# Centring a weight with SCALAR_TENSOR_TENSOR in place of TENSOR_TENSOR, and the builder's estimates with it

## The chip, the cores and the metric

The kernel runs on one core of a Trainium2 chip. The metric is the device time of one execution in microseconds (us), the median of several runs. A profile of one execution shows what each engine did: PE (matmuls; PEld, its weight loads), DVE (VectorE), ACT (ScalarE), POOL (GpSimd), and SP, which issues most of the DMAs.

## What is computed

Nystrom attention over 8 batches of 8 heads (576 tokens, head size 64, 32 landmarks), followed by a normalised two-layer network with a residual. Cut to what matters:

```python
A, Bm, C = softmax(q @ k_lm.T), softmax(q_lm @ k_lm.T), softmax(q_lm @ k.T)
Z = Bm.T / (norm1(Bm) * norminf(Bm) + 1e-6)
for _ in range(6):
    Z = 2 * Z - Z @ Bm @ Z
x = heads_side_by_side(A @ Z @ C @ v)              # 8 x 576 x 512
xn = (x - mean(x)) / sqrt(var(x) + 1e-6) * g_ln
out = x + relu(xn @ w_ch1) @ w_ch2                 # 512 -> 2048 -> 512
```

The mean of x is never taken off x. It is taken off the weight: from each column of W1 (already scaled by g_ln) its mean over the 512 inputs is subtracted. This is "centring W1".

## The kernel before

**Tiling.** Tokens stand in 36 blocks of 128. W1 is held as `w1_16`, f16, 128 partitions by 4 input chunks by 2048; W2 as `w2_16`. The first layer of a batch has 16 chunks `m` of 128 hidden units (`First.chunk`), each 8 matmuls of 288 columns into a PSUM tile `psh`, and ACT or DVE writes its relu as `hT`. The second layer has 16 matmuls of 512 columns for each block (`bank<-w,hT` in the profile), and DVE writes them scaled and added into `xblk`; from batch 4 on seven products of half size take the place of eight.

**Centring.** The negative column means come from matmuls with a constant (`less_mean`, L1111) and lie as f16 tiles `less`. For batches 0 and 1, whose first layers come before the weight is centred, the means are added later, into the product `m16` (L1151 to L1157). When batch 1 takes its four products, `whole.extend` (L1159) puts eight jobs in a list: four column groups `f`, each in two halves of two input chunks. `center_w1(f, c)` (L1123) does one of them: one DVE instruction over 128x1024 f16, in place, `w1_16 + less`. Batches from 2 on use the centred weight. In the profile these are the rows `w<-w,less`.

**POOL's work beside it.** For each tile of q and k of a later batch POOL casts the staged f32 data to f16 (`nat`, 128x1152). For some of them it also makes landmark sums, in three halving sums `asum` and a last one `s`: four instructions behind the cast, here called a chain (`Coming.cast`, L778). DVE transposes `s` to `sT` and reduces it to `part`, and PE spreads `part` over the heads (`part,spread`) for the next attention. POOL also multiplies the exponentials of q's scores by their reciprocal sums (`normalize`, L512, rows `ea<-ea,lns`), and casts v (`natv`). PE uses `ea` in the matmuls `zcbd,ea` and in `psh<-ea,m`.

**What sets the order.** All engines run instructions in the order in which they are issued, and this order is made when the kernel is built. Four streams of work (attentions, first layers, rows of batch 0, second layers) are generators that say from when their next piece could run. `run` (L1512) takes the first that is ready by the clock of the builder, and `help_out` (L1427) puts side work between: loads, POOL's casts and chains, DVE's transposes, `center_w1` (L1467), measuring, stores. The clock is a set of estimates: `Clock.took` (L124) says how long an instruction takes on its engine, `Clock.note` (L146) moves the time at which the engine is free. For a DVE instruction over 1024 elements the estimate is 1080 ns (L141). When such an instruction writes `w1_16`, POOL's time of being free is also moved, by 430 ns (L205, with the names in `parted_w1`, L374). The estimates are used when the order is made and nowhere else; on the chip only semaphores hold an instruction.

A helper issues nearly all instructions, so most rows of the profile have its line: L268 for DVE, ACT and POOL, L274 for the matmuls. Rows are told apart by tile names.

## Time and profile before

| | |
|---|---|
| median of 3 runs | 281.72 us (281.32 to 282.81) |
| the profiled execution | 282.81 us, its span 281.0 us |
| PE, DVE, ACT, POOL busy | 266.2, 212.3, 161.9, 160.1 us |
| granted TensorE clock | 0.997 of full speed |
| `w<-w,less` on DVE | 8 instructions, 7.1 us, from 69.3 to 78.2 us |

The span goes from the first to the last instruction that the profile shows; the 1.8 us beside it lie around them. A row of a group gives engine, operation, output and inputs by tile name, their shapes and the count, then the busy time in us, the mean of one in ns, and the idle time of the engine just before, with what ended it. A row of the timeline gives start and length in us and merges equal neighbours. A row of a stretch gives its limits, its length, the busy time and count for PE, PEld, DVE, ACT and POOL, then granted clock, DMA share and GB/s.

### The profile page before, as it was taken

The numbers are of one execution on the slowest core, as the hardware profiler recorded it, in microseconds if no ns is written. First come the engines' busy times: TensorE is split into PE (matmuls) and PEld (weight loads), VectorE is DVE, ScalarE is ACT, GpSimd is POOL, SyncE is SP. The second block draws the span as 40 slices with busy tenths as digits, with TensorE's granted clock in tenths as the row PEclk, the third lists the DMA queues.
The fourth block names the chain that finished last, engine by engine and source line by source line (L and its number), as shares of the span: only waits on it lengthen the run. The fifth ranks groups of instructions, "written<-read, shape, count | busy, mean of one in ns | idle before, by whom it ended". The sixth has DMA issues, their size and how long they took to land.

```text
span 281.0 us, 8678 instructions
## 1 busy us (share of the span) xinstructions
PE 266.2 (95%) x3618; PEld 165.6 (59%) x3618; DVE 212.3 (76%) x479; ACT 161.9 (58%) x287; POOL 160.1 (57%) x187
## 2 busy tenths in 40 slices
PE   7988999999999999889989999999999999999994
PEld 7744554355444564344555645567877666678883
DVE  3558985999999847888978384697885499748761
ACT  2676954368554887148889754698248733671000
POOL 5368778999999999978999999310000040100000
PEclk9999999999999999999999999999999999999998
DMA  7999999989745579893750101310060005300606
GB/s 244 384 387 388 388 388 392 354 278 266 246 126 160 152 249 304 265 279 95 221 188 2 34 8 45 72 40 0 2 144 9 1 5 118 72 0 2 149 22 167
DMA packets 23375, 46.70 MB, mean 166 GB/s; under 512 B 2212, under 2 KB 2472, under 8 KB 23336
## 3 DMA queue, kind: packets, MB, share of 16 engines
q1 hardware_dynamic: 23176, 46.02, 51.9%
q8 instruction: 28, 0.46, 0.7%
q10 hardware_dynamic: 160, 0.13, 0.2%
q14 instruction: 11, 0.09, 0.1%
HBM read 36.70 MB, written 9.44 MB: 164 GB/s over the span
## 4 chain that ended last, share of the span: by engine, by line
PE 79%; DVE 9%; ACT 5%; issue 3%; DMA 2%; SPq 0%; DVEq 0%; ACTq 0%
PE bank L274 51%; PE psh L274 21%; DMA stg<-in_q_dram 2%; ACT hT L268 2%; DVE xblk L268 2%; PE pscv L274 2%; DVE m L268 2%; DVE xT L268 1%; PE psec L274 1%; PE psd L274 1%; DVE part L268 1%; ACT ec L268 1%; DVE hT L268 1%; ACT lns L268 1%; PE psea L274 1%
## 5 line engine op out<-in xcount | busy, mean ns | idle before, releaser
L274 PE MATMUL bank<-w,hT 128*128 128x512 f16 (+1 forms) x528 | 109.2, 335 | 1.1 <-issue 1.0
L268 ACT ACTIVATE hT<-psh 128x576 f16<-128x576 f32 x115 | 71.0, 652 | 17.4 <-PE psh L274 16.0
L274 PE MATMUL psh<-ea,m 128*128 128x288 f16 x512 | 76.9, 286 | 2.8 <-ACT hT L268 2.1
L274 PEld LDWEIGHTS <-hT 128*128 128x128 f16 x656 | 60.4, 98 | 32.2 <-issue 6.9
L274 PEld LDWEIGHTS <-m 128*128 128x128 f16 x512 | 47.9, 97 | 25.3 <-issue 10.1
L268 DVE SCALAR_TENSOR_TENSOR xblk<-bank,rstd,xblk 128x256 f32<-128x256 f32 (+1 forms) x77 | 39.2, 541 | 18.2 <-PE bank L274 18.2
L268 POOL TENSOR_TENSOR ea<-ea,lns 128x576 f16<-128x576 f16 x14 | 18.1, 1306 | 47.2 <-ACT lns L268 47.0
L268 POOL CAST nat<-stg 128x1152 f16<-128x1152 f32 x28 | 32.6, 1181 | 2.0 <-DMA stg<-in_k_dram 1.1
L268 POOL CAST natv<-stg 64x1152 f16<-64x1152 f32 (+1 forms) x23 | 26.7, 1161 | 8.8 <-DMA stg<-in_v_dram 7.9
L268 ACT COPY xblk<-bank 128x512 f32<-128x512 f32 (+1 forms) x34 | 19.1, 588 | 12.2 <-PE bank L274 12.0
L268 DVE BATCH_NORM_STATS2 six<-xblk 128x6 f32<-128x512 f32 x36 | 24.2, 671 | 0.0
L268 ACT CAST m<-bank 128x512 f16<-128x512 f32 x30 | 17.0, 588 | 9.9 <-PE bank L274 9.9
L268 DVE STREAM_TRANSPOSE xT<-nat 128x576 uint32<-128x576 uint32 x28 | 21.4, 765 | 0.6 <-POOL nat L268 0.6
L268 ACT ACTIVATE lns<-psd 128x576 f32<-128x576 f32 x16 | 10.3, 646 | 17.8 <-PE psd L274 16.7
L268 DVE TENSOR_REDUCE part<-xT 128x32 f16<-128x576 f16 x28 | 20.0, 742 | 0.2
L268 POOL TENSOR_TENSOR asum<-asum 128x256 f32<-128x256 f32 (+1 forms) x28 | 18.0, 644 | 2.2
L268 DVE CAST m<-bank 128x512 f16<-128x512 f32 x18 | 12.2, 679 | 7.3 <-PE bank L274 7.2
L268 POOL TENSOR_TENSOR asum<-nat 128x512 f32<-128x512 f16 x14 | 16.5, 1178 | 1.1
L274 PE MATMUL bank<-w2mix,hT 128*128 128x256 f16 x128 | 16.5, 273 | 0.0
L274 PE MATMUL bank<-w2mix 128*128 128x256 f16 x128 | 16.0, 273 | 0.0
L268 DVE SCALAR_TENSOR_TENSOR st<-st,bank 128x128 f16<-128x128 f16 (+2 forms) x36 | 11.1, 308 | 6.4 <-PE bank L274 6.0
L274 PE MATMUL bank<-zcbd,ea 128*128 128x256 f16 (+1 forms) x80 | 14.4, 275 | 1.0 <-DVE m L268 0.8
(123 smaller groups left out, 341.6 us busy)
## 6 DMA issues: line engine op xcount, KB each, us to landing
stg<-in_q_dram SPq DMA_DIRECT2D x16, 576.0 KB, 5.7
stg<-in_k_dram SPq DMA_DIRECT2D x16, 576.0 KB, 5.4
stg<-in_v_dram SPq DMA_DIRECT2D x16, 576.0 KB, 7.1
out_dram<-xblk SPq DMA_DIRECT2D x70, 128.0 KB, 2.3
wstg<-in_moe_w_ch_dram SPq DMA_DIRECT2D x16, 512.0 KB, 7.1
out_dram<-xblk ACTq DMA_DIRECT2D x2, 64.0 KB, 2.3
out_dram<-xblk SPq DMA_DIRECT2D x2, 64.0 KB, 2.1
g_rows<-in_moe_g_ln_dram SPq DMA_DIRECT2D x1, 2.0 KB
```

Source lines behind the costliest of these rows:

```text
L268: return lambda *args, **kw: keep(getattr(self.engine, op)(*args, **kw))
L274: keep(nc.tensor.matmul(o, l, r, start=start, stop=stop, tile_position=(rb, cb), skip_group_check=(skip or cb != 0)))
```

## The change

One instruction is written in another way: the same in-place sum, as SCALAR_TENSOR_TENSOR, that is `(w1_16 * 1.0) + less`. The builder's estimate of a DVE instruction over 1024 elements goes from 1080 to 1200 ns. The charge of 430 ns to POOL goes, and the set of names that served it. The second-layer mixes keep their own estimate of 690.

```diff
-    parted, mixed_, parted_w1 = {}, set(), set()
+    parted, mixed_ = {}, set()
...
             if n == 1024:
-                return 690 if name_of(i.outs[0].bass_ap) in mixed_ else 1080
+                return 690 if name_of(i.outs[0].bass_ap) in mixed_ else 1200
...
                 self.free[e] = done - self.OVERLAP[e]
-                if e == 'DVE' and count[0] == 1024 and writes[0] in parted_w1:
-                    self.free['Pool'] = max(self.free['Pool'], start) + 430
...
-    parted_w1.update(f"{w1_16.name}:{i}" for i in range(KCH * MCH))
...
         o = w1_16[:, ds(c, 2), ts(f, 512)]
-        dve.tensor_tensor(out=o, in0=o, in1=less(f)[:, None, :].broadcast_to([P, 2, 512]),
-                          op=ALU.add)
+        dve.scalar_tensor_tensor(out=o, in0=o, scalar=1.0,
+                                 in1=less(f)[:, None, :].broadcast_to([P, 2, 512]),
+                                 op0=ALU.mult, op1=ALU.add)
```

Since the estimates set the order, the order of all five engines differs from the first of these instructions on, in places.

## The prediction

> **What bounds the kernel now.** I read the busy table and the chain that ended last, then the busy times by stretch and the waits of 69 to 106 us, where the edited instructions lie, and then DVE and POOL there in order of time.

> ```profile
> PE 266.2 (95%) x3618; PEld 165.6 (59%) x3618; DVE 212.3 (76%) x479; ACT 161.9 (58%) x287; POOL 160.1 (57%) x187
> PE 79%; DVE 9%; ACT 5%; issue 3%; DMA 2%; SPq 0%; DVEq 0%; ACTq 0%
> ...
> 69.00:82.00 13.00, 12.69 (x245) 6.19 (x243) 12.40 (x28) 7.82 (x15) 12.21 (x13) 1.00 0.69 216
> 82.00:94.00 12.00, 12.00 (x111) 5.55 (x104) 10.81 (x27) 6.12 (x13) 11.29 (x15) 1.00 0.52 163
> ```

> PE is the bound: 95% of the span and 79% of the chain. In the last two rows (stretch, its length, then PE, weight loads, DVE, ACT, POOL) PE is full, but so are DVE (12.40 of 13.00) and POOL (12.21). POOL is nowhere in the chain: it is just in time. So a faster POOL gains little by itself, and a later DVE or POOL shows once its margin is gone. PE issues in a fixed order, so a late operand stops everything behind it.

> The edited instructions, and POOL beside them:

> ```profile
> L268 DVE TENSOR_TENSOR w<-w,less 128x1024 f16<-128x1024 f16 x8 | 7.1, 922 | 0.0
> L268 DVE TENSOR_TENSOR w2mix<-w2mix,hT 128x1024 f16<-128x1024 f16 x8 | 5.4, 681 | 0.0
> L268 DVE SCALAR_TENSOR_TENSOR xblk<-bank,rstd,xblk 128x512 f32<-128x512 f32 x19 | 13.9, 737 | 6.0 <-PE bank L274 6.0
> ...
> 69.35 3.49 DVE L268 TENSOR_TENSOR w<-w,less 128x1024 f16<-128x1024 f16 x4
> ...
> 69.43 2.02 POOL L268 TENSOR_TENSOR asum<-asum 128x256 f32<-128x256 f32 x2
> 71.53 0.75 POOL L268 TENSOR_TENSOR s<-asum,nat 128x128 f16<-128x128 f32 x1
> 72.23 1.60 POOL L268 CAST nat<-stg 128x1152 f16<-128x1152 f32 x1
> ...
> 80.91 1.26 POOL L268 TENSOR_TENSOR asum<-asum 128x256 f32<-128x256 f32 x2
> 82.24 0.43 POOL L268 TENSOR_TENSOR s<-asum,nat 128x128 f16<-128x128 f32 x1
> 82.63 2.52 POOL L268 TENSOR_TENSOR ea<-ea,lns 128x576 f16<-128x576 f16 x2
> ```

> The same DVE shape takes 681 ns on w2mix, with POOL nearly idle, and 922 on W1. POOL's pair of sums takes 2.02 us beside the W1 adds and 1.26 later, the last sum 0.75 against 0.43. The two engines block each other in turns. Over all eight adds POOL loses 0.76 + 0.32 + 0.46 + 0.72 + 0.56 + 0.33 = 3.15 us.

> **The change, part by part.**

> *The instruction.* Eight TENSOR_TENSOR go, eight SCALAR_TENSOR_TENSOR of 128x1024 come, both big operands in SBUF. The trace has none like that. Bounds: below, 681 ns, if it still takes two f16 elements at a time; above, the slope of SCALAR_TENSOR_TENSOR with a PSUM operand, 477 ns for 256 and 737 for 512, so 1.016 ns an element and 737 + 520 = 1257 ns for 1024. The f16 form with PSUM (732 for 512, 476 for 256) has the same slope. I take 1257: all rows of this operation lie on that line. That is 0.575 us more for each.

> [...]

> *Does it hold POOL?* Bounds: no hold at all, or for its whole length. The nearest row is not the W1 add but an add that goes one element at a time, also with two SBUF operands:

> ```profile
> 21.95 1.20 POOL L268 TENSOR_SCALAR w<-wstg,g_sb 128x512 f16<-128x512 f32 x1
> ...
> 21.86 0.81 DVE L268 TENSOR_TENSOR ea<-ea,lns 128x288 f16<-128x288 f16 x2
> ```

> Two such adds last from 21.86 to 22.67 (450 ns for 288 elements each, the slow rate). POOL's scaling, which elsewhere takes 0.69, takes 1.20 beside them: it ends 0.48 after the second add. So the slow rate does not spare POOL, and I take a hold for the whole length. [...]

> With the hold, each of the eight POOL instructions beside W1 is released 0.575 us later: 8 x 0.575 = **4.6 us** that POOL is later than before at 82.6.

> *The order.* The estimate goes from 1080 to 1200 and the 430 that POOL was charged for each add is gone, so the builder believes POOL to be earlier. Set side by side, the two built orders hold the same PE instructions, as many as before; up to the W1 adds nothing moves. Three moves matter. (1) On POOL the two ea products of batch 2 stood behind two sum chains (cast, three sums, last sum); now a third chain stands ahead of them. That chain lasts from 85.09 to 89.26, **4.17 us**. (2) On PE the last part/spread pair before batches 3 and 4 moves up to behind 12 psh matmuls. (3) One adding of W1 and the transposes change places on DVE, and PE's w2 matmuls are shared out anew between the six iterations. Loads and stores on SP change places from the same region on; their transfers are not in the chain there, so I cost them at nothing. If that cover fails a load of 5.4 us could show.

> *What PE then waits for.* The ea products end at 85.15 before; now at 85.15 + 4.6 + 4.17 = 93.9. PE wants them (times from its rows in order of time) at the first zcbd,ea matmul: 88.80 before, and one w2 matmul (0.22) more ahead of it now, 89.0. **Stall 4.9 us.**

> Next, POOL has two chains of 4.17 to the last sum that part needs: 93.9 + 8.3 = 102.2; transpose 0.23, reduce 0.28 and 0.13 to PE (reduce ended at 100.30, PE began at 100.43) make 102.85. PE, from zcbd at 93.9, needs 4.49 to the first w1 group (88.80 to 93.29 before, the same matmuls), then 0.34 + 0.99 (8 psh) + 0.87 (4 w2) + 0.49 (4 psh), which is 101.1. **Stall 1.75 us.**

> DVE itself is late too: the first four take 4 x 1.18 (1257 less the usual 0.08 overlap) in place of 3.49 less 0.06 and wait for POOL between them as now (1.1 us), so rsum starts at 69.35 + 4.72 + 1.1, about 75.1 and not 72.78. PE's gram follows rsum by 1.23 as before, 76.3, where PE is there after 7 w2 matmuls, 72.98 + 7 x 0.216 = 74.5: 1.8 late. In the iterations behind it each added instruction and its wait for POOL (1.2 to 1.6 us) stands ahead of one st, and PE has 4 to 8 w2 matmuls (0.9 to 1.7) to cover it; following both lists on, I find 0.4, 0.1 and 0.3 more. So PE is late by some 2.6 us at pszt. This lies ahead of the ea wait and within it: PE must wait until 93.9 anyway. So nothing is added; if the ea wait went, these 2.6 would show instead.

> Sum: 4.9 + 1.75 = 6.65, about **6.6 us**. Behind 106 us POOL is 4.4 us late and PE 6.6, so POOL has margin again (it waited 1.94 for lns at 127). The profiled execution took 282.81 with a span of 281.0; with 6.6 it would be 289.4. The median of the three runs is 281.72: forecast **288.3**.

> Both ends of this case: if each hold grows by 0.4 and not 0.575, POOL is 1.4 less late and so is PE: 286.9. If each grows by 0.3 more, since DVE keeps POOL waiting over its own start, 2.4 more: 290.7.

> **Rivals.**

> *No hold, slow instruction.* POOL gets its 3.15 us back, ea ends at 86.2 and never shows. DVE remains: without POOL's waits rsum starts at 69.35 + 4.72 = 74.07, 1.29 later; gram is ready at 75.3 and PE is there at 74.5: 0.8. The first iteration then waits 0.2 (78.1 against 77.9), the second 0.3 (80.2 against 79.9), the fourth 0.2: 1.5 us in all, **283.2**. For: the trace has no such operation with two SBUF operands. Against: the ea row.

> *The added instruction is like the old one* (681 ns, same hold). Then the order alone acts: ea at 85.15 + 4.17 = 89.3 against 89.0, and part/spread 1.75: 2.0 us, **283.7**. Against: every row of this operation has the slow slope.

> *Not slower: POOL freed and instruction waits gone.* Between 106 and 130 us PE waits 1.20 + 0.49 + 0.99 = 2.68 us for "issue", nothing that the profile names, while DMA is busy 0.82. If there is no hold, casts free the staging buffers 3 us sooner, loads end sooner, and if those waits come from that traffic they go: 1.5 - 2.68 = -1.2, **280.5**; where the iterations' 1.5 hides in the new sharing of w2 matmuls too, 279.0. It decides from no hold on, that is POOL's pair back at 1.26. For: DVE gives POOL back 3 us. Against: POOL is not in the chain.

> **How the numbers follow.** Chances: hold 0.60, no hold 0.18, like the old 0.06, freed 0.16. About 0.5%, 1.4 us, is what can be told from no change. Slower: 0.60 + 0.06 + half of 0.18 = 0.75. Same: the other half and 0.06 of the freed case, 0.15. Faster: 0.10 of it. The range leaves out the faster end of the freed case and some of the far end: 281.3 to 290.7. The forecast case alone is 286.9 to 290.7.

> **What would show it.** W1 rows near 1.26 us or more, not 0.68; POOL's pair of sums beside them about 3 us, not 2.02 (1.26 would end the forecast's case); PE idle of several us ahead of zcbd,ea released by POOL ea, and one ahead of part/spread. Wrong it would be if POOL's rows there are at their plain lengths, or if PE has no wait for POOL between 85 and 106 us.

## The result, and the profile after

The changed kernel takes **292.19 us** (median of six runs, 290.09 to 294.27) against 281.95 for the kernel before on the same chip (six runs, 281.32 to 284.31): ratio 1.034 [1.028, 1.041], slower. Forecast was 288.3 with a range to 290.7: the direction was right, and the time lies 1.5 us above the range. The profiled execution took 294.27 us with a span of 292.5, and a granted clock of 0.986 (the six runs had 0.986, 0.988, 0.986, 0.998, 0.994, 0.994).

The page of the changed kernel, busy times and the chain that ended last, and between them the granted clock in 40 slices:

```profile
PE 269.3 (92%) x3618; PEld 165.4 (57%) x3618; DVE 216.0 (74%) x478; ACT 162.9 (56%) x288; POOL 164.3 (56%) x187
...
PEclk9999999999999999995999999999999999999999
...
PE 59%; DVE 15%; POOL 12%; issue 5%; ACT 5%; DMA 2%; SPq 0%; POOLq 0%; ACTq 0%; DVEq 0%
```

PE is busy for 3.1 us more and the span is 11.5 us longer: 8.4 us are PE's idle time. POOL, which was not in the chain before, now has 12% of it. And one slice, at 132 to 139 us, has the clock at about half. Before had no such slice ahead of its last:

```profile
PEclk9999999999999999999999999999999999999998
```

DVE's added instruction and POOL beside it, in order of time:

```profile
70.13 5.62 DVE L266 SCALAR_TENSOR_TENSOR w<-w,less 128x1024 f16<-128x1024 f16 x4
...
70.20 3.10 POOL L266 TENSOR_TENSOR asum<-asum 128x256 f32<-128x256 f32 x2
73.38 1.29 POOL L266 TENSOR_TENSOR s<-asum,nat 128x128 f16<-128x128 f32 x1
74.61 2.13 POOL L266 CAST nat<-stg 128x1152 f16<-128x1152 f32 x1
...
91.84 2.52 POOL L266 TENSOR_TENSOR ea<-ea,lns 128x576 f16<-128x576 f16 x2
```

The first four adds last 5.62 us (3.49 before). POOL's pair of sums takes 3.10 (2.02 before, 1.26 undisturbed), the last sum 1.29 (0.75), the cast 2.13 (1.60). Over all eight adds POOL loses 7.44 us against 3.15 before. The ea products end at 94.36. This execution was already 0.78 us late when the first add began (70.13 against 69.35, ahead of anything that the change touches), and this is taken off below.

PE's rows with a wait, of the same kernel (the wait and who ended it stand in brackets):

```profile
76.39 0.19 PE L272 MATMUL bank<-st,bones 128*128 128x64 f16 x1 [1.02 <-DVE st L266]
...
93.18 0.28 PE L272 MATMUL bank<-zcbd,ea 128*128 128x256 f16 x1 [0.93 <-POOL ea L266]
...
94.42 0.28 PE L272 MATMUL bank<-zcbd,ea 128*128 128x256 f16 x1 [0.96 <-POOL ea L266]
...
103.34 0.38 PE L272 MATMUL bank<-part,spread 128*128 128x256 f16 x2 [1.68 <-DVE part L266]
...
131.92 3.57 PE L272 MATMUL bank<-w,hT 128*128 128x512 f16 x8 [2.96 <-issue]
```

The first four are where the prediction put them (a fifth wait for st, 0.55 us at 79.71, is left out here). The last is not: 2.96 us in which PE waits for nothing that the profile names. The kernel before has three waits of that kind, 2.68 us in all:

```profile
115.19 0.32 PE L274 MATMUL psea<-xT,lm 32*32 32x288 f16 x8 [1.20 <-issue]
119.74 0.29 PE L274 MATMUL bank<-st 32*32 32x64 f16 x15 [0.49 <-issue]
124.02 1.46 PE L274 MATMUL bank<-w,hT 128*128 128x512 f16 x6 [0.99 <-issue]
```

The wait of 2.96 us follows a stretch of short matmuls, and behind it the eight matmuls take 3.57 us, begun 0.427 us apart, where 8 x 0.216 = 1.7 is usual (0.216 apart again behind 137.8): they run at half clock. Stretches around it (limits, length, busy time and count of PE, PEld, DVE, ACT, POOL, granted clock, DMA share, GB/s):

```profile
127.40:130.80 3.40, 1.40 (x22) 0.65 (x21) 3.30 (x11) 2.39 (x4) 3.19 (x4) 1.00 1.00 308
130.80:134.20 3.40, 2.28 (x6) 0.84 (x6) 1.17 (x2) 0.00 (x0) 3.24 (x5) 0.50 0.58 202
134.20:137.70 3.50, 3.50 (x12) 1.47 (x10) 2.59 (x4) 1.60 (x3) 1.60 (x3) 0.51 0.18 42
```

The clock records of the trace give the limits: half clock from 130.83 to 137.66 us, that is twice 3.41. In the 3.4 us ahead of it PE was busy for 1.40.

Where the time went, by PE's time at the same place in both programs, less 0.78:

| place | later than before | forecast |
|---|---|---|
| behind the second wait for ea | 4.7 us | 4.9 |
| first matmul of the attention of batches 3 and 4 (113.77 against 105.72) | 7.3 us | 6.6 |
| last matmul | 10.7 us | 6.6 |

### The profile page after: what moved, and what is told of

Its sections match the earlier page's. It is cut to its first block, busy times and chain, and to the rows that moved or that the text cites. A ratio compares the mean times of both kernels' runs of the same rounds, so it can differ in the third digit from the quotient of the medians.

```text
span 292.5 us, 8688 instructions
## 1 busy us (share of the span) xinstructions
PE 269.3 (92%) x3618; PEld 165.4 (57%) x3618; DVE 216.0 (74%) x478; ACT 162.9 (56%) x288; POOL 164.3 (56%) x187
## 4 chain that ended last, share of the span: by engine, by line
PE 59%; DVE 15%; POOL 12%; issue 5%; ACT 5%; DMA 2%; SPq 0%; POOLq 0%; ACTq 0%; DVEq 0%
PE bank L272 39%; PE psh L272 16%; POOL asum L266 6%; POOL nat L266 3%; DVE xT L266 2%; DMA stg<-in_q_dram 2%; DVE part L266 2%; DVE m L266 2%; DVE xblk L266 2%; ACT hT L266 2%; DVE st L266 1%; ACT ec L266 1%; DVE hT L266 1%; POOL s L266 1%; PE psd L272 1%
## 5 line engine op out<-in xcount | busy, mean ns | idle before, releaser
L272 PE MATMUL bank<-w,hT 128*128 128x512 f16 (+1 forms) x528 | 110.5, 340 | 3.0 <-issue 3.0
L272 PEld LDWEIGHTS <-hT 128*128 128x128 f16 x656 | 60.9, 99 | 35.1 <-issue 10.2
L272 PE MATMUL psh<-ea,m 128*128 128x288 f16 x512 | 76.3, 286 | 3.9 <-ACT hT L266 2.2
L272 PEld LDWEIGHTS <-m 128*128 128x128 f16 x512 | 48.0, 97 | 26.4 <-issue 11.5
L266 POOL CAST nat<-stg 128x1152 f16<-128x1152 f32 x28 | 33.6, 1219 | 2.8 <-DMA stg<-in_k_dram 1.9
L266 POOL TENSOR_TENSOR asum<-asum 128x256 f32<-128x256 f32 (+1 forms) x28 | 20.2, 720 | 2.2
L266 DVE CAST m<-bank 128x512 f16<-128x512 f32 x17 | 11.6, 683 | 9.4 <-PE bank L272 8.2
L266 POOL TENSOR_TENSOR asum<-nat 128x512 f32<-128x512 f16 x14 | 17.0, 1217 | 1.1
```

The costliest lines, as they stand in the source:

```text
L266: return lambda *args, **kw: keep(getattr(self.engine, op)(*args, **kw))
L272: keep(nc.tensor.matmul(o, l, r, start=start, stop=stop, tile_position=(rb, cb), skip_group_check=(skip or cb != 0)))
```

## The experiments

Theory: POOL is held for the whole length of each add, and PE meets what POOL owes at ea and at part (the forecast's case). Rivals: the slow rate on DVE does it, or the order alone, or loads that hold up PE's instructions. All ratios are to the kernel before on the same chip; its median there was 282.92 for the first four, 283.66 for the next four, 282.72 for the next four and 282.14 for the last two.

| run | what | median (us) | ratio |
|---|---|---|---|
| e1_stt_old_order | instruction alone | 286.71 | 1.012 [1.004, 1.020] |
| e2_tt_new_order | order alone | 287.27 | 1.013 [1.007, 1.020] |
| e3_stt_told | instruction, longer estimates | 287.94 | 1.016 [1.008, 1.024] |
| e5_after_light | changed, lighter loads at 70 to 95 us | 290.70 | 1.030 [1.022, 1.038] |
| e6_before_light | before, the same | 281.81 | 0.996 [0.993, 0.999] |
| e7_after_ea_first | changed, ea ahead of the third chain | 295.51 | 1.043 [1.035, 1.051] |
| e8_tt_told | before, nearer estimates | 286.50 | 1.011 [1.002, 1.021] |
| e9_after_light2 | changed, lighter loads at 113 to 131 us | 291.34 | 1.034 [1.027, 1.040] |
| e10_before_light2 | before, the same | 281.55 | 0.997 [0.994, 1.000] |
| e11_after_spread_late | changed, part,spread later | 291.80 | 1.034 [1.027, 1.041] |
| e12_before_gate | before, loads held back | 282.39 | 0.999 [0.997, 1.002] |
| e13_light2_fill | e9 with PE's waits filled | 292.06 | 1.036 [1.031, 1.040] |
| e14_stt_from_psum | changed, mean read from PSUM | 284.52 | 1.009 [1.006, 1.012] |

### The instruction alone, the order alone

```diff
 e1: the kernel before, its estimates and its order, and
-        dve.tensor_tensor(out=o, in0=o, in1=less(f)..., op=ALU.add)
+        dve.scalar_tensor_tensor(out=o, in0=o, scalar=1.0, in1=less(f)..., op0=ALU.mult, op1=ALU.add)
 e2: the changed kernel, its estimates and its order, and the same edit backwards
```

Expected of e1:

> SCALAR_TENSOR_TENSOR in the order of the kernel before: the builder keeps its old estimates, so PE, POOL, ACT and SP have the same lists as before and DVE differs in the eight instructions alone. Theory A (the instruction holds POOL for its whole length, and the order, made as if it did not, puts ea behind one chain too many): the instruction alone makes POOL 4.3 us later (7.4 us of holds in place of 3.15), ea ends at about 89.5 where PE wants it at 88.8, the last part comes 2.2 us late, and rsum some 3 us late; as these lie one behind the other, not added, about +3 us, 285. Rival B (the instruction is all, the order does not matter): +8 to +10, as the changed kernel, 290 to 292. Rival C (the order is all): within 1 us of before. If PE idles for over 2 us in one piece ahead of gram and the granted clock falls to half for it, 2 to 3 us come on top in A.

Expected of e2:

> TENSOR_TENSOR as before, in the order of the changed kernel: PE, POOL, ACT and SP have the same lists as the changed kernel. Theory A: POOL loses 3.15 us as before, ea ends at 85.15 + 4.17 = 89.3 against 89.0 and part/spread costs 1.75 at most, so +1 to +2 us, 283 to 284, if the issue wait near 129 us does not come; if that wait and the halved clock behind it belong to this order and its loads, they come here too and it is +5, 287. Rival B (instruction is all): within 1 us of before. Rival C (order is all): +8 to +10.

Measured: +1.2% and +1.3%, by the medians 3.8 and 4.3 us; both together cost 10.2. So neither half is the cause alone. That both together cost more than the sum of the two (8.1) lies within the error of these ratios; what the traces show is that PE waits for ea in the changed kernel and in neither half. The instruction in the old order makes PE wait for DVE only, ahead of 103 us:

```profile
76.11 0.19 PE L274 MATMUL bank<-st,bones 128*128 128x64 f16 x1 [1.45 <-DVE st L268]
79.43 0.23 PE L274 MATMUL bank<-st 32*32 32x64 f16 x6 [0.77 <-DVE st L268]
84.83 0.24 PE L274 MATMUL bank<-st 32*32 32x64 f16 x8 [1.05 <-DVE st L268]
```

No wait of PE names POOL: ea stands behind two chains there, ends at 89.93, and PE asks for it at 93.26. Theory A had put these waits for ea and part into this run too, and was wrong in that; what the instruction costs here is DVE's lateness, 3.27 us in these three waits. In the new order with the old instruction PE waits for part alone, 1.68 us, and for ea not at all:

```profile
98.34 0.38 PE L272 MATMUL bank<-part,spread 128*128 128x256 f16 x2 [1.68 <-DVE part L266]
```

### Longer and nearer estimates

```diff
 e3: e1, with the estimates
-                return 690 if name_of(i.outs[0].bass_ap) in mixed_ else 1080
+                return 690 if name_of(i.outs[0].bass_ap) in mixed_ else 1440
-                    self.free['Pool'] = max(self.free['Pool'], start) + 430
+                    self.free['Pool'] = max(self.free['Pool'], start) + 930
 e8: the kernel before, with 920 for 1080 and 390 for 430
```

Expected of e3:

> SCALAR_TENSOR_TENSOR, with a builder that is told what the trace of the changed kernel shows: 1440 ns on DVE (spacing 1.36 us and 0.08 of overlap) and 930 ns of POOL's time for each. Theory A: the work is the same, but ea stands ahead of the third chain again and PE gets more w2 matmuls where DVE is late, so most of the loss goes: +1 to +4 us, 283 to 286. Rival B (the instruction is all): 290 or more, as the changed kernel.

Expected of e8:

> The kernel before (TENSOR_TENSOR) with estimates that fit what its profile shows: 920 in place of 1080 for the add, and 390 in place of 430 for what POOL loses. If the order of before is worth its time because its estimates lie near the measured ones, this is the same or a little better: 281 to 283.5. If any other order loses some us by new meetings of PE with late operands, as in the kernel with the new order and the old instruction (+3.7): 284 to 287.

Measured: telling the builder what the added instruction costs (e3) ends within the error of e1, and above the 283 to 286 that theory A gave. And estimates that lie nearer to the measured lengths of the old one (e8) make the kernel slower by 1.1%: the second guess was right. An estimate here chooses one order among many; a truer one does not choose a better one by itself.

### The disputed instructions by themselves

The rest of the computation is left out; six instructions of each kind over 128x1024 f16, alone and beside POOL casts of the same size.

> Only the disputed instructions, the rest of the computation is left out: six additions over 128x1024 f16 in each stage, alone or beside six POOL casts of 128x1024 f32 to f16 or six POOL memsets. If two SBUF operands make the hold: TENSOR_TENSOR 0.68 us alone, SCALAR_TENSOR_TENSOR 1.2 alone, both and the additions of an f32 operand much longer beside casts and the casts longer than alone (1.04), but SCALAR_TENSOR_TENSOR with its second operand in PSUM 1.25 and the casts at their plain length. If the rate makes the hold (two elements at a time), only TENSOR_TENSOR of f16 disturbs casts and SCALAR_TENSOR_TENSOR does not. Beside memsets, which read nothing, no disturbance if the hold is of reads alone.

Groups of that run (tt is TENSOR_TENSOR, st SCALAR_TENSOR_TENSOR with two SBUF operands, sp with the second operand in PSUM; _d on DVE, _p the casts beside it, c in the name means with casts):

```profile
L51 DVE TENSOR_TENSOR tt_d<-tt_d,less 128x1024 f16<-128x1024 f16 x6 | 3.7, 684 | 0.0
L53 DVE SCALAR_TENSOR_TENSOR st_d<-st_d,less 128x1024 f16<-128x1024 f16 x6 | 6.9, 1217 | 0.0
...
L53 DVE SCALAR_TENSOR_TENSOR stc_d<-stc_d,less 128x1024 f16<-128x1024 f16 x6 | 11.8, 2034 | 0.0
L67 POOL CAST stc_p<-raw 128x1024 f16<-128x1024 f32 x6 | 10.9, 1863 | 0.0
...
L53 DVE SCALAR_TENSOR_TENSOR spc_d<-spc_d,inps 128x1024 f16<-128x1024 f16 x6 | 6.9, 1212 | 0.0
L67 POOL CAST spc_p<-raw 128x1024 f16<-128x1024 f32 x6 | 5.9, 1036 | 0.0
```

Alone, 684 against 1217 ns. Beside POOL casts (1035 alone) the added form takes 2034 and the casts 1863: an add loses 0.82 us and a cast 0.83. The old form beside casts takes 1502 and the casts 1420, so it holds too, but for a shorter time (0.39 us for a cast). With the mean in PSUM the same operation at the same rate takes 1212 and the casts 1036: no hold. A TENSOR_TENSOR whose second operand is f32 behaved as the added form, 2034 and 1863; it was not run alone. So in this run the hold comes with two operands in SBUF, and it is longer with the slower form (0.83 us for a cast against 0.39).

### POOL's hold taken away, the rate kept

```diff
+        bank = banks.take([P, 512])
+        MM(bank, ident16[:], less(f))
         dve.scalar_tensor_tensor(out=o, in0=o, scalar=1.0,
-                                 in1=less(f)[:, None, :].broadcast_to([P, 2, 512]),
+                                 in1=bank[:, None, :].broadcast_to([P, 2, 512]),
```

> The changed kernel, in which each of the eight SCALAR_TENSOR_TENSOR takes the mean from PSUM, where a matmul with the identity (0.22 us each, 1.7 in all) puts it just ahead; the rest of the edit, the estimates and POOL's order up to the attention of batches 3 and 4 stay. By the run of the instructions alone such an add lasts 1.21 us as now, but does not hold POOL (POOL cast 1036 ns beside it, 1863 beside the form with two SBUF operands). Theory G (POOL's hold decides, as the forecast has it: 4.6 us of POOL's debt is met at ea and part): POOL's pair of sums at 1.26 us beside the adds, no wait of PE for POOL ea, and at part at most 0.5; DVE late by some 1.5 at most; with 1.7 of added matmuls, in part within waits, 284.5 to 287. Rival H (the slow rate on DVE decides and the hold is secondary): the waits for DVE st stay near 2.5 to 3.3 and the time is 288 to 290.

Measured: 284.52 us, 0.9% above the kernel before on its chip where the changed kernel was 3.4% above on its own, although PE has 1.7 us of matmuls more. First the group of the adds, then DVE's and POOL's rows in order of time:

```profile
L266 DVE SCALAR_TENSOR_TENSOR w<-w,bank 128x1024 f16<-128x1024 f16 x8 | 9.5, 1208 | 0.1
```

```profile
69.88 4.66 DVE L266 SCALAR_TENSOR_TENSOR w<-w,bank 128x1024 f16<-128x1024 f16 x4
...
69.95 1.26 POOL L266 TENSOR_TENSOR asum<-asum 128x256 f32<-128x256 f32 x2
71.29 0.43 POOL L266 TENSOR_TENSOR s<-asum,nat 128x128 f16<-128x128 f32 x1
```

The adds are as slow as ever (1208 ns), and POOL's pair is back at 1.26. PE has no wait for POOL ea, for part or for DVE st between 69 and 107 us. This speaks for theory G and against rival H: at the same rate and without the hold, PE waits for none of them. Three things are to be kept in mind. The hold goes on both sides (DVE's four adds last 4.66 us and not 5.62), and the 3.15 us that POOL lost in the kernel before go too. PE's order is not quite that of the changed kernel, since the builder places the added matmuls; but ea ends at 86.70 here and PE asks for it at 91.17, so by an estimate with the 7.44 us that POOL loses in the changed kernel it would end at 94.1, and PE would wait in this order as well. The form of e14 is also the one that the changed estimates describe: 1200 ns, and nothing charged to POOL.

### One debt or two: ea first, part later

```diff
 e7: the third chain's cast waits for the ea products of batch 2
-            if i not in self.stg:
+            if i not in self.stg or (self.bs == (3, 4) and i == 5 and len(normed) < 4):
 e11: the last part,spread pair waits for more of PE's work
-            if any(i < done for _, i, *_ in self.jobs):
+            if any(i < done for _, i, *_ in self.jobs) or (self.bs == (3, 4) and y == 1 and clock.count < 1250):
```

Expected of e7:

> The changed kernel with one edit to POOL's order: the third sum chain waits until both ea products of batch 2 are out, as in the kernel before. Theory C (the ea wait and the part wait are one debt: POOL is late at the end of its last chain, and PE meets it at part if not at ea): the wait at zcbd,ea falls from 4.9 to under 1 (DVE's lateness of about 2.5 shows ahead of it), the wait at part,spread grows from 1.7 to about 3.5 to 4, PE is behind part at the same time within 0.7 us, and the time is within 1 us of the changed kernel (289 to 292). Rival D (the order of ea costs its 4.2 us by itself): the ea wait goes, DVE's 2.5 shows in its place, the part wait stays below 2: 2 to 2.5 us less, 287.5 to 289.5.

Measured in e7, PE's only wait between 84 and 106 us:

```profile
103.09 0.38 PE L272 MATMUL bank<-part,spread 128*128 128x256 f16 x2 [3.41 <-DVE part L266]
```

With ea ahead of the third chain the two waits for it (0.93 and 0.96) are gone, and the wait for part has grown from 1.68 to 3.41. PE is behind it at 103.09, at 103.34 in the changed kernel; counted from the same psh matmul ahead of the adds (69.89 and 70.14) both are 33.20 us. Theory C holds: POOL's debt is one sum, and it falls due at whichever of its products PE asks for. (The time was not within 1 us: the median is 3 us higher, ratio 1.043 against 1.034, and the profiled execution has an issue wait of 4.19 us and a half clock behind 125 us, of which more below.)

Expected of e11:

> The changed kernel with one edit to PE's order: the last part,spread pair ahead of batches 3 and 4 goes 28 matmuls (about 4 us) further back, near its place in the kernel before; POOL and SP keep their order. Theory C (one debt of POOL, met at ea and at part): the ea wait of 4.9 stays, the part wait of 1.7 goes, since PE comes to it 4 us later and part is ready: 1.7 us less than the changed kernel's 290 to 292, 288.3 to 290.5 as far as the waits behind 113 us let it show; PE is 1.5 to 2 us earlier at 106 us. Rival D (what POOL owes shows somewhere whatever PE's order): the wait moves to the next use of the pair, the attention of batches 3 and 4, and PE is not earlier at 114 us.

Measured in e11, DVE's rows, and then PE's next wait:

```profile
102.48 0.24 DVE L266 STREAM_TRANSPOSE sT<-s 128x64 uint32<-128x64 uint32 x1 [2.30 <-POOL s L266]
...
105.37 0.72 DVE L266 TENSOR_SCALAR hT<-psh 128x576 f16<-128x576 f32 x1
```

```profile
106.15 0.65 PE L272 MATMUL psh<-ea,m 128*128 128x288 f16 x4 [1.72 <-DVE hT L266]
```

Here theory C failed and rival D was nearer. PE comes to part when it is ready, but DVE had stood 2.30 us at the transpose of POOL's sum, with its relu `hT` behind it, and PE waits 1.72 us for that. The first matmul of the attention of batches 3 and 4 comes at 113.5, as without the edit (113.8).

### Loads and the wait named issue

The trace has 28 packets of 16 KB on the queue that the profile names instruction. PE has 7242 instructions (3618 matmuls, 3618 weight loads, 6 others): by an estimate one packet for each 256. The four issue waits above all end at a place 193 instructions past a multiple of 256 (behind 3009, 3265 and 3521 instructions in the kernel before, 3521 in the changed one), 1.61, 1.36, 1.37 and 1.51 us after such a packet had landed. In the changed kernel PE passed the place before that, 3265, at 125.76 us; the next packet began at 129.53, 3.77 later, while loads held the DMA engines at 95%, and landed at 130.41; PE resumed at 131.92. Behind 150 us, where few loads run, each packet begins within 1.6 us of such a place, on either side of it. The theory was that loads cause the wait, and that the wait is what the forecast lacked.

```diff
 e5, e6: v of batches 3 and 4, k of batch 5; e9, e10: v of batches 5 and 6, k of batch 7
-            out=t[:],
+            out=t[0:few(src, b)],          # 4 of 128 partitions for these tiles
```

Expected of e5 and e6:

> The changed kernel with the same order on all engines, but six loads made light: the four v tiles of batches 3 and 4 and the first two k tiles of batch 5 fetch 4 of 128 partitions, and POOL's casts of them read a constant tile of zeros in their place (so these batches' results are wrong). Nothing else moves 576 KB between 114 and 132 us. Theory A (PE's wait named issue is a fetch of instructions that stands behind these loads, and the half clock follows from a PE idle that long): the wait of 2.96 us ahead of the matmul at PE row 3519 falls to 0.6 or less, no half clock behind it, the profiled span about 287.5 to 289 in place of 292.5, median 288 to 290. Theory B (the wait is PE's own, or of the order, and the loads have nothing to do with it): the wait stays above 2 us, median 290 to 293. In both the waits for POOL ea (5.0 in all over before) and for part (1.7) stay, since POOL's order and lengths stay.

> The kernel before with the same six loads made light in the same way, as the control for it. Theory A: its own issue waits behind 114 us (0.49 and 0.99) go, the one at 114 us (1.20), which follows the loads of q and k, stays: 1 to 1.5 us less than before, about 281.5 against 282.9. Theory B: no difference, within 0.5 us. What the changed kernel gains by light loads beyond what this one gains is the share of the loads in the difference between the two.

Both missed their aim: loads run two batches further ahead than I had assumed, so bytes were taken away at 70 to 95 us. The issue wait in e5 stayed, at 1.68 us (no matmul began between 128.56 and 130.41). In e6 the issue waits of the kernel before are gone all the same, and the median is 0.4% lower. They were repeated with the right tiles.

> The runs with light loads of the v tiles of batches 3 and 4 took bytes away from 70 to 95 us, not from 113 to 131: loads run two batches further ahead than was assumed there. This one repeats it with the right tiles: in the changed kernel the v tiles of batches 5 and 6 and the first two k tiles of batch 7 fetch 4 of 128 partitions, and POOL's casts of them read a tile of zeros (their results are wrong). Order on all engines as in the changed kernel. Theory A (the issue wait is a fetch of instructions behind these loads): the fetch for the block that ends at PE row 3519 starts within 1.5 us of the crossing that asks for it (3.77 in the changed kernel, 4.94 and 2.65 in two others of this order), PE's wait there is at most 0.8 us (2.96), no half clock behind it, and the median is 287 to 289. Theory B (the wait is PE's own): still 1.8 us or more, 290 to 293. The waits for ea (5) and part (1.7) stay in both.

> The control: the kernel before with the same six loads light. Theory A: its issue waits of 0.49 and 0.99 behind 114 us fall to 0.3 or less each, the one at 114 us (1.20) stays since the q and k loads ahead of it stay: 281 to 282, and less spread between runs than the kernel before has (281.2 to 286.3). Theory B: as before, 282 to 284 with its spread.

In e9 the packet began 0.03 us after its place, and PE has no issue wait at all. But its median, 291.34, is that of the changed kernel: theory A is right on the wait and wrong on its price. PE meets other late operands a few us on:

```profile
133.23 0.30 PE L272 MATMUL pszt<-st,cv 32*64 32x32 f16 x16 [0.78 <-ACT lns L266]
134.49 0.25 PE L272 MATMUL pszc<-cv,st 32*32 32x64 f16 x16 [0.95 <-ACT lns L266]
```

and three of its four runs had a clock below 0.997 (the profiled one, the fastest, had 0.999). The control e10 gained as little (0.3%); its issue waits are gone as in e6, and PE waits 0.90 us for lns instead (0.86 in e6). So these six loads have no part that can be seen in the difference between the two kernels. They do steady the kernel before: 9 of 10 runs of e6 and 8 of 10 of e10 had a clock of 0.997 or more, against 6 of 12 and 12 of 17 of the kernel before beside them. A version meant to beat both followed from the same thought:

```diff
 e12: the kernel before
-                            and clock.wire <= now + AHEAD):
+                            and clock.wire <= now + AHEAD
+                            and not 1360 <= clock.count < 1790):
```

> A version meant to beat both, on theory A: the kernel before, TENSOR_TENSOR, in which no load is issued while PE is between its matmuls 1360 and 1790, the stretch of short matmuls in which a block of instructions lasts 3 to 6 us; the v loads of batches 5 and 6 come behind it. All is computed. The order behind that stretch changes. If the fetches come in time and nothing new is late: waits behind 114 us from 2.7 to about 1.2 us, 280 to 282. If the later loads make POOL's casts late or the new order meets late operands as the other new orders did: 283 to 287.

Measured 0.999 [0.997, 1.002]: one issue wait is left, of 0.17 us, and what that saves is lost in waits for lns, xblk and hT from 126 to 140 us (0.56, 0.40, 0.28, 0.56 and 0.47). No kernel of this study is faster than the one before with all the work done.

### The halved clock

```diff
 e13: e9, with matmuls of zeros where PE waits
+    fill(8)    ahead of the first zcbd,ea of batches 2 and 3
+    fill(14)   ahead of the last part,spread
+    fill(7)    ahead of pszt and of pszc of batches 3 and 4
```

> The changed kernel with the six loads of 113 to 131 us light (as in the second run with light loads; their results are wrong) and 44 matmuls of zeros (128x256, 0.11 us each) put where PE waits anyway: 8 ahead of the first zcbd,ea of batch 2, 14 ahead of the last part,spread, 7 each ahead of pszt and pszc of batches 3 and 4, 8 ahead of their first zcbd,ea. Nothing else moves. So far 4 of 18 runs of kernels with the changed order had a granted clock of 0.997 or more, and these four took 289.8 to 290.4 us; the other 14 took up to 295. Theory E (the clock is halved for some 3.41 us after a stretch of 3.41 us in which the array did too little, so idle PE is paid for a second time by luck of where the stretches begin): with the idle filled, most runs have 0.997 or more and the median is 289.5 to 291. Rival F (the halving does not come from idle PE in these places): clocks as before, one in four at 0.997 or more, median 291 to 293.

Measured: five of six runs had a clock of 0.997 or more, where it had been 4 of 18 with this order (the changed kernel, e5, e9, and e11, which differs in one pair). This speaks for theory E but does not settle it: e13 ran on another chip than e5, e9 and e11, and the kernel before kept its clock more often there too (the table's last rows). The median did not fall, and lies above the 289.5 to 291 that theory E gave: the 44 matmuls take some 5.4 us (22 of them 2.73), more than the waits that they fill, and the five full-clock runs took 291.5 to 292.6.

| kernel | runs at 0.997 or more | their times (us) |
|---|---|---|
| changed, e5, e9, e11 | 4 of 18 | 289.75 to 290.35 |
| e1 | 4 of 4 | 285.4 to 288.8 |
| e14 | 8 of 9 | 284.2 to 286.0 |
| before, beside e5 | 6 of 12 | 281.2 to 284.3 |
| before, beside e9 and e11 | 12 of 17 | 281.1 to 283.4 |
| before, beside e13 and e14 | 12 of 14 | 281.1 to 283.6 |

The clock is not all that differs between runs: with the full clock e1 takes from 285.4 to 288.8 us, and the kernel before from 281.2 to 284.3 beside e5.

## Why the prediction missed

**The instruction's length: right.** Forecast 1257 ns from the slope of the PSUM form, measured 1217 alone and 1208 in the kernel (e14). That all rows of the operation lie on that line was not so: `st<-st,bank` takes 276 ns for 128 elements and 416 for 256, where the line gives 347 and 477; its slope of 1.09 ns an element is near. The 681 ns row was no guide; whether its form takes two elements at a time, as the lower bound had it, no run shows, only that it takes 684 ns alone.

**The hold: right, and it decides.** Forecast 4.6 us more for POOL, measured 7.44 - 3.15 = 4.29; without any hold (e14) PE has no wait for POOL there. The run of the instructions alone agrees: cast 1863 ns beside two SBUF operands and 1036 beside one. POOL memsets, which only write, were not held in that run (953 ns beside the two-operand form, 952 without it). What makes one engine wait for the other there is not shown.

**The order: right.** The ea products were to end at 93.9 and ended at 94.36 - 0.78 = 93.6; PE behind them was to be 4.9 late and was 4.7. The stall at part was to be 1.75 and was 1.68. DVE's lateness, said to lie within the ea wait, does so: PE waits 1.02 and 0.55 at st and is 2.5 late at pszt (90.02 less 0.78, against 86.72), where 2.6 was forecast; e7 shows that taking the ea wait away moves the debt to part.

**The sum behind 106 us: 6.6 against 7.3.** The sum took the two stalls for all there is. Beyond them the runs show 0.9: half of it are two waits for ACT's hT at 110.87 and 112.25 us (0.25 and 0.20), which the kernel before does not have there; the rest no row names.

**The step that failed** is the last: "Behind 106 us POOL is 4.4 us late and PE 6.6, so POOL has margin again", that is, a sum that ends there. From there to the end 3.4 us more came. In the profiled execution 2.9 of them are the half clock (5.74 us, from 131.92 to 137.66, of work at half speed), and 0.3 the issue wait beyond what before had (2.96 against 1.20 + 0.49 + 0.99). The forecast has no term for the clock. It priced each stall of PE once; here 2.9 us of half clock came on top, behind a stretch in which PE was busy for 1.40 of 3.4 us. The loads, costed "at nothing", were priced rightly as far as e9 and e10 can tell.

The changed kernel's one run with a full clock took 290.10 us (289.75 to 290.35 with e5, e9 and e11), 1.8 above the forecast and inside its range; 0.7 of that is the shortfall of the sum above, if it is the same there as in the profiled execution; for the rest there is no trace of that run. The other five runs had a lower clock, and four of them took 291.7 to 294.3; the fifth, at 0.994, took 290.09. So the clock is the likely reason that the median lies above the range. A half clock behind a PE wait is seen in the one profiled run; for the others it is inferred, from e13 above all, and stays open.

Of the rivals, *no hold, slow instruction* was priced at 283.2; that case was built as e14 and takes 284.52 with 1.7 us of added matmuls. *The order alone* (the added instruction like the old one) was priced at 283.7 and took 287.27 (285.64 and 286.26 in its two full-clock runs, 288.3 in the two others): the part wait came as forecast, 1.68 us, the ea wait of 0.3 did not, and what makes the rest is not shown. *Freed*, priced at 280.5, did not come: with POOL free in e14, issue waits of 0.56 and 2.02 us remain.

## What to carry to other kernels

Before an elementwise instruction is exchanged for one with another rate, look at what other engines do beside it and where its operands lie: here the longer hold of POOL (4.29 us over eight adds) cost more than the longer instruction, and one operand in PSUM took the hold away (a cast beside it 1036 ns and not 1863). A debt of an engine that is just in time is one sum: moving one of its products ahead moves the wait to the next product (here part, from 1.68 to 3.41 us), or to whatever stands behind it in another engine's queue (1.72 us for hT). And price idle PE with the clock in mind: here waits that left PE idle for 2.0 of 3.4 us were followed by half clock, which cost 2.9 us more.

## What the hardware showed that was not expected

**PE stood until a packet of instructions had landed.** The four waits named issue end 1.4 to 1.6 us behind such a packet, at the same place of a block of 256, and with lighter loads (e9) the packet began 0.03 us after its place and the wait was gone. The wait was long where a block lasts 3 us: 256 short matmuls and weight loads took 3.0 us in the changed kernel (125.76 to 128.79), and PE stood for 2.96. So it is not semaphores alone that hold an instruction on the chip, as the text ahead of the prediction had it: here a packet that came late held PE, and DVE and POOL held each other (2034 and 1863 ns side by side, 1217 and 1035 alone).
